# Twelve expert blocks moved into the attention stage, and the order of the loads fixed

## The chip, the cores and the metric

One core of one Trainium2 chip. The metric is the device time of the whole program in microseconds (us). A time quoted for a kernel is the median of its runs.

The engines are named as in the profile: PE is TensorE, PEld its weight loads, DVE is VectorE, ACT is ScalarE, POOL is GpSimd, SP is SyncE. The "granted clock" of a stretch is the share of TensorE's full clock that the profile records as let through: 1.00 is full, 0.50 is half. L144 is line 144 of that kernel's file, so the same operation has another line number in each kernel; go by the names of the tiles.

## The reference, cut to what matters

```python
# attention: batch 8, heads 8, sequence 576, head size 64
scores = scale * q @ k.T                      # per batch and head
scores = where(0 <= i - j < 128, scores + alibi_bias, -1e9)
x = (softmax(scores) @ v)  -> reshaped to (4608 tokens, 512)

# routing: 8 rounds that normalise rows and columns of P
P = exp(x @ w_gate - max)                     # (4608, 8)
for _ in range(8):
    P /= P.sum(1); P /= P.sum(0); P *= 4608 / 8

# every expert sees every token
for e in range(8):
    out += P[:, e:e+1] * (relu(x @ w1[e]) @ w2[e])   # 512 -> 1024 -> 512
```

Three properties carry the argument. An expert needs x, but not P, until its result is added up. P needs all tokens, because of the column sums. And the experts are by far the larger part: 8 experts x 4608 tokens.

## The kernel before

Loads. Each batch's q and k are cast to fp16 into a staging area in DRAM (three areas, used in turn), then read back transposed; v is cast straight into SBUF.

```python
def stage(b):
    sl = b % NST                                         # NST = 3
    nc.gpsimd.dma_start(out=q16[sl]..., in_=q[b]...)     # cast
    nc.gpsimd.dma_start(out=k16[sl]..., in_=k[b]...)     # cast
    vsb = asb.tile([P, NKB, H, Dh + 2], FP16, tag="vsb", bufs=3)
    for kb in range(NKB):
        nc.gpsimd.dma_start(out=vsb[0:nk, kb, :, 0:Dh], in_=v[b, ...])
    ...
    nc.sync.dma_start(out=QT, in_=q16[sl], transpose=True)
    nc.sync.dma_start(out=KT, in_=k16[sl], transpose=True)

stage(0); stage(1)
for b in range(B):
    if b + 2 < B: stage(b + 2)
    if b == B - 4: prefetch_weights(0)
    if b == B - 1: prefetch_weights(1)
    ...
```

The scheduler may reorder instructions within an engine's queue where data allow it, and it did so with these loads.

Attention, per batch and key block (five key blocks a batch; cut): 8 score matmuls of a 64-row array tile, exp on ScalarE, mask on VectorE, up to 16 value matmuls, division by the row sum, 4 transposes into `xT`; at the end of a batch the gate.

```python
for j in range(4):
    for hb in range(2):
        nc.tensor.matmul(out=ps[0:nk, hb, 0:nq], lhsT=KT[64*hb:64*hb+64, ...], rhs=QT[64*hb:64*hb+64, ...])   # psS
...
for i, (hh, lhsT, rhs) in enumerate(ops):
    nc.tensor.matmul(out=psN[0:nqb, hh, :], lhsT=lhsT, rhs=rhs, ...)
...
for dc in range(NDT):
    nc.tensor.matmul(out=psXT[:, dc, 0:nqb], lhsT=xsb[...], rhs=ident[...], is_transpose=True, ...)
```

Then the eight routing rounds (VectorE and GpSimd), then the experts: per expert nine blocks of 512 tokens, each 32 matmuls of the first layer (`psh`) and 32 of the second (`psy`), all 128x512, and the sum in `acc`:

```python
for e in range(E):
    for g in range(NG):
        ...                                    # psh -> relu on ACT -> hT; psy
        if e == 0: acc = psy * P_sb[:, blk, 0:1]          # VectorE
        else:      acc = psy * P_sb[:, blk, e:e+1] + acc  # VectorE
```

The softmax here doesn't subtract the row's maximum and nothing guards it: scores larger than these inputs give would overflow.

Of the kernel before, what the change touches and what calls it, by code (L numbers as in the profile page):

```python
# [9 lines left out]
FP16 = mybir.dt.float16  # L10
# [4 lines left out]
def kernel(  # L15
# [39 lines left out]
    NST = 3  # L55
    q16 = nc.dram_tensor("q16_i", [NST, S, HD], FP16, kind="Internal").ap()
    k16 = nc.dram_tensor("k16_i", [NST, S, HD], FP16, kind="Internal").ap()

    per = ctx.enter_context(tc.tile_pool(name="per", bufs=1))
    xT = per.tile([P, NDT, Ntok], FP16, name="xT")  # L60
    P_sb = per.tile([P, NBLK, E], FP32, name="P_sb")
# [14 lines left out]
    def prefetch_weights(e: int):  # L76
        w1t = per.tile([P, NDT, Fd], FP16, name=f"w1t_{e}", tag="w1t", bufs=2)
        w2t = per.tile([P, NFT, HD], FP16, name=f"w2t_{e}", tag="w2t", bufs=2)
        nc.gpsimd.dma_start(out=w1t, in_=moe_w1[e].rearrange("(dt p) f -> p dt f", p=P))  # L79
        nc.gpsimd.dma_start(out=w2t, in_=moe_w2[e].rearrange("(ft p) d -> p ft d", p=P))  # L80
        w1ts[e] = w1t
        w2ts[e] = w2t

    gate_done = 0

    with (
# [3 lines left out]
        staged: dict = {}  # L90

        def stage(b: int):
            sl = b % NST
            nc.gpsimd.dma_start(  # L94
                out=q16[sl].rearrange("s (h d) -> s h d", d=Dh),
# [3 lines left out]
                out=k16[sl].rearrange("s (h d) -> s h d", d=Dh),  # L99
                in_=k[b].rearrange("h s d -> s h d"),  # L100
            )
            vsb = asb.tile([P, NKB, H, Dh + 2], FP16, name=f"vsb_{b}", tag="vsb", bufs=3)
# [8 lines left out]
            QT = asb.tile([P, NDT, S], FP16, name=f"QT_{b}", tag="QT", bufs=3)  # L111
            KT = asb.tile([P, NDT, S], FP16, name=f"KT_{b}", tag="KT", bufs=3)
            nc.sync.dma_start(out=QT, in_=q16[sl], transpose=True)  # L113
            nc.sync.dma_start(out=KT, in_=k16[sl], transpose=True)
            staged[b] = (vsb, QT, KT)

        stage(0)
        stage(1)
        for b in range(B):
            if b + 2 < B:  # L120
                stage(b + 2)
            vsb, QT, KT = staged.pop(b)
            if b == B - 4:
                prefetch_weights(0)
            if b == B - 1:
                prefetch_weights(1)

            pt_prev = None
            for kb in range(NKB):
# [6 lines left out]
                for j in range(4):  # L136
# [12 lines left out]
                    psS.append(ps)  # L149

# [25 lines left out]

                xsb = asb.tile([P, H, Dh], FP16, name=f"xsb_{b}_{kb}", tag="xsb", bufs=2)
# [35 lines left out]
                psXT = aps.tile([P, NDT, P], FP16, name=f"psXT_{b}_{kb}", tag="psXT")  # L213
# [14 lines left out]
            for blk in range(gate_done, done):  # L228
                psG = aps.tile([P, E], FP32, name=f"psG_{blk}", tag="psG")
# [10 lines left out]

        for _ in range(8):
# [22 lines left out]
    with (  # L264
        tc.tile_pool(name="msb", bufs=1) as msb,
        tc.tile_pool(name="mps", bufs=1, space=bass.MemoryType.PSUM) as mps,
    ):
        acc = msb.tile([P, NBLK, HD], FP32, name="acc")
        for e in range(E):
            if 1 <= e and e + 1 < E:  # L270
                prefetch_weights(e + 1)
            w1t = w1ts[e]
# [3 lines left out]
            def emit_l1(g, e=e, w1t=w1t, hTs=hTs):  # L276
                hT = msb.tile([P, NFT, GT], FP16, name=f"hT_{e}_{g}", tag="hT", bufs=2)
                for ft in range(NFT):
                    psh = mps.tile([P, GT], FP32, name=f"psh_{e}_{g}_{ft}", tag="psh", bufs=2)
                    for dt in range(NDT):  # L280
                        nc.tensor.matmul(  # L281
                            out=psh,
                            lhsT=w1t[:, dt, P * ft : P * ft + P],
                            rhs=xT[:, dt, GT * g : GT * g + GT],
                            start=(dt == 0),
                            stop=(dt == NDT - 1),
                        )
                    nc.scalar.activation(out=hT[:, ft, :], in_=psh, func=AF.Relu)  # L288
                hTs[g] = hT

            def emit_l2(g, e=e, w2t=w2t, hTs=hTs):
                hT = hTs.pop(g)
                for ms in range(4):
                    blk = 4 * g + ms
                    psy = mps.tile([P, HD], FP32, name=f"psy_{e}_{blk}", tag="psy", bufs=3)
# [8 lines left out]
                    if e == 0:  # L304
                        nc.vector.tensor_scalar(  # L305
                            out=acc[:, blk, :],
                            in0=psy,
                            scalar1=P_sb[:, blk, 0:1],
                            scalar2=None,
                            op0=ALU.mult,  # L310
                        )
                    else:
                        nc.vector.scalar_tensor_tensor(  # L313
                            out=acc[:, blk, :],
                            in0=psy,
                            scalar=P_sb[:, blk, e : e + 1],
                            in1=acc[:, blk, :],
                            op0=ALU.mult,
                            op1=ALU.add,
                        )  # L320
# [6 lines left out]
            for g in range(NG):  # L327
                if g + 1 < NG:
                    emit_l1(g + 1)
                emit_l2(g)  # L330
# [30 lines left out]
```

## Time and profile before

| | |
|---|---|
| median of 4 runs | 1241.53 us (1238.02 to 1244.81) |
| profiled execution | span 1241.1 us |
| attention and loads | 0 to 229 us |
| routing rounds and the first expert blocks | 229 to 257 us |
| dense expert matmuls | to 1241 us, 216.2 ns each |

The prediction below shows the views that it rests on.

```profile
PE 1141.7 (92%) x5808; PEld 532.6 (43%) x5808; DVE 334.9 (27%) x704; ACT 427.4 (34%) x773; POOL 86.3 (7%) x85
...
L144 PE MATMUL psS<-QT,KT 64*128 64x256 f16 (+2 forms) x320 | 72.4, 349 | 41.9 <-DMA KT<-k_i 36.5
L195 PE MATMUL psN<-vsb,pt 128*128 128x65 f16 (+2 forms) x576 | 64.1, 246 | 46.3 <-DMA vsb<-in_v_dram 46.2
```

Keep two numbers in mind: PE is busy 1141.7 us with 5808 instructions, and a score matmul takes 349 ns on average.

### The profile page before, as it was taken

The page shows a single profiled execution, that of the slowest core. Times are in us where ns is not written, and L with a number is a line of the kernel's source. Part 1 is how long each engine was busy: PE and PEld are TensorE (multiplying, and loading weights), DVE is VectorE, ACT ScalarE, POOL GpSimd, SP SyncE. Part 2 cuts the span into 40 slices and gives each one's busy share as a digit, 9 for nine tenths or more (in the row PEclk, how much of TensorE's full clock was granted, in tenths as well). Part 3 has the DMA queues.
Part 4 walks back from the last instruction along what each step waited for, and adds up shares of the span by engine and source line. Part 5 has one row for each costly group of instructions (what it writes and reads, how often), then busy time and mean ns, then how long its engine had stood idle before and what let it go on. Part 6 is the DMA issues. An engine that isn't in the chain of part 4 may idle for free.

```text
span 1241.1 us, 13876 instructions
## 1 busy us (share of the span) xinstructions
PE 1141.7 (92%) x5808; PEld 532.6 (43%) x5808; DVE 334.9 (27%) x704; ACT 427.4 (34%) x773; POOL 86.3 (7%) x85
## 2 busy tenths in 40 slices
PE   0880589989999999999999999999999999999998
PEld 0450355434444444444444444444444444444443
DVE  0560366731221122112211221122111211121112
ACT  1440355423333333333233323332333233323331
POOL 6431330000000000000000000000000000000000
PEclk9999999989999999999999999999999999999999
DMA  9999995000040004000300030003100310001212
GB/s 146 153 154 139 157 146 25 2 1 1 1 67 2 1 1 62 8 1 1 58 11 1 1 55 14 1 1 49 20 1 1 47 23 1 1 1 60 77 68 102
DMA packets 167471, 51.27 MB, mean 41 GB/s; under 512 B 150384, under 2 KB 158576, under 8 KB 167408
## 3 DMA queue, kind: packets, MB, share of 16 engines
q0 software_dynamic: 124560, 30.95, 28.6%
q1 hardware_dynamic: 42848, 19.44, 9.2%
q8 instruction: 45, 0.74, 0.3%
q14 instruction: 18, 0.15, 0.0%
HBM read 62.44 MB, written 18.87 MB: 66 GB/s over the span
## 4 chain that ended last, share of the span: by engine, by line
PE 84%; DMA 9%; DVE 2%; issue 2%; ACT 1%; POOL 1%; SPq 0%; DVEq 0%; POOLq 0%; ACTq 0%
PE psy L297 40%; PE psh L281 39%; DMA vsb<-in_v_dram 7%; PE psS L144 2%; PE psN L195 2%; DMA q_i<-in_q_dram 2%; PE psXT L215 1%; DMA KT<-k_i 1%; ACT e L156 1%; SPq L113 0%; DVE cs_sb L250 0%; PE psG L231 0%; DVE P_sb L244 0%; DVE rs_sb L242 0%; POOL ca_sb L253 0%
## 5 line engine op out<-in xcount | busy, mean ns | idle before, releaser
L288 ACT ACTIVATE hT<-psh 128x512 f16<-128x512 f32 x576 | 343.8, 597 | 650.9 <-PE psh L281 635.4
L297 PE MATMUL psy<-w2t,hT 128*128 128x512 f16 x2304 | 510.4, 380 | 5.8 <-DVE acc L305 5.8
L281 PE MATMUL psh<-xT,w1t 128*128 128x512 f16 x2304 | 512.9, 380 | 0.4 <-ACT P_sb L238 0.3
L313 DVE SCALAR_TENSOR_TENSOR acc<-psy,P_sb,acc 128x512 f32<-128x512 f32 x252 | 189.2, 751 | 683.9 <-PE psy L297 683.9
L297 PEld LDWEIGHTS <-hT 128*128 128x128 f16 x2304 | 225.4, 98 | 279.7 <-issue 8.5
L281 PEld LDWEIGHTS <-w1t 128*128 128x128 f16 x2304 | 225.1, 98 | 277.7 <-issue 14.6
L156 ACT ACTIVATE e<-psS 128x512 f16<-128x512 f32 (+2 forms) x160 | 77.2, 510 | 106.6 <-PE psS L144 96.4
L144 PE MATMUL psS<-QT,KT 64*128 64x256 f16 (+2 forms) x320 | 72.4, 349 | 41.9 <-DMA KT<-k_i 36.5
L195 PE MATMUL psN<-vsb,pt 128*128 128x65 f16 (+2 forms) x576 | 64.1, 246 | 46.3 <-DMA vsb<-in_v_dram 46.2
L195 PEld LDWEIGHTS <-pt 128*128 128x128 f16 (+2 forms) x576 | 44.3, 132 | 69.8 <-issue 56.4
L169 DVE TENSOR_TENSOR pt<-e,maskT 128x512 f16<-128x512 f16 (+2 forms) x160 | 52.5, 355 | 28.4 <-ACT e L156 28.3
L79 POOL DMA_DIRECT2D w1t<-in_moe_w_dram x8 | 6.6, 826 | 648.4 <-PE psh L281 645.3
L305 DVE TENSOR_SCALAR acc<-psy,P_sb 128x512 f32<-128x512 f32 x36 | 26.8, 750 | 82.2 <-PE psy L297 81.8
L144 PEld LDWEIGHTS <-KT 64*128 64x128 f16 (+1 forms) x320 | 22.4, 106 | 56.9 <-DMA KT<-k_i 36.9
L106 POOL DMA_DIRECT2D vsb<-in_v_dram x40 | 35.7, 1053 | 49.2 <-DMA q_i<-in_q_dram 16.6
L224 DVE COPY xT<-psXT 128x512 f16<-128x512 f16 (+1 forms) x40 | 15.9, 398 | 73.6 <-PE psS L144 51.3
L206 DVE TENSOR_TENSOR xsb<-psN,rden 128x256 f16<-128x256 f32 (+1 forms) x80 | 31.3, 408 | 0.1
L215 PE MATMUL psXT<-ident,xsb 128*128 128x128 f16 (+1 forms) x160 | 30.2, 290 | 0.8 <-DVE xsb L206 0.8
L205 DVE RECIPROCAL rden<-psN 128x4 f32<-128x4 f32 (+1 forms) x80 | 14.1, 177 | 27.7 <-PE psN L195 27.5
L98 POOL DMA_DIRECT2D k_i<-in_k_dram x8 | 18.1, 2263 | 32.6 <-issue 17.6
L94 POOL DMA_DIRECT2D q_i<-in_q_dram x8 | 17.9, 2244 | 26.7 <-issue 18.7
L238 ACT ACTIVATE P_sb<-psG 128x8 f32<-128x8 f32 x36 | 6.4, 177 | 38.4 <-PE psG L231 37.6
(18 smaller groups left out, 64.0 us busy)
## 6 DMA issues: line engine op xcount, KB each, us to landing
out_dram<-acc SPq DMA_DIRECT2D x36, 256.0 KB, 2.0
w1t<-in_moe_w_dram POOLq DMA_DIRECT2D x8, 1024.0 KB, 8.2
w2t<-in_moe_w_dram POOLq DMA_DIRECT2D x8, 1024.0 KB, 9.2
q_i<-in_q_dram POOLq DMA_DIRECT2D x8, 576.0 KB, 20.6
k_i<-in_k_dram POOLq DMA_DIRECT2D x8, 576.0 KB, 19.3
vsb<-in_v_dram POOLq DMA_DIRECT2D x32, 128.0 KB, 18.6
maskT<-maskT_c SPq DMA_DIRECT2D x1, 512.0 KB, 3.3
vsb<-in_v_dram POOLq DMA_DIRECT2D x8, 64.0 KB, 17.8
```

What stands on the lines that cost most here:

```text
L106: nc.gpsimd.dma_start(out=vsb[0:nk, kb, :, 0:Dh], in_=v[b, :, k0 : k0 + nk, :].rearrange("h s d -> s h d"),)
L144: nc.tensor.matmul(out=ps[0:nk, hb, 0:nq], lhsT=KT[64 * hb : 64 * hb + 64, j, k0 : k0 + nk], rhs=QT[64 * hb : 64 * hb + 64, j, k0 : k0 + nq],)
L156: nc.scalar.activation(out=e4[0:nk, :, 0:nq], in_=psS[j][0:nk, :, 0:nq], func=AF.Exp, scale=scale,)
L169: nc.vector.tensor_tensor(out=ptj[0:nk, :, 0:nq], in0=e4s[j][0:nk, :, 0:nq], in1=maskT[0:nk, 2 * j : 2 * j + 2, 0:nq], op=ALU.mult,)
L195: nc.tensor.matmul(out=psN[0:nqb, hh, :], lhsT=lhsT, rhs=rhs, start=(i == 0), stop=(i == len(ops) - 1),)
L206: nc.vector.tensor_tensor(out=xsb[0:nqb, 4 * hg : 4 * hg + 4, :], in0=psN[0:nqb, :, 0:Dh], in1=rden[0:nqb, :].unsqueeze(2).to_broadcast([n ...
L215: nc.tensor.matmul(out=psXT[:, dc, 0:nqb], lhsT=xsb[0:nqb, 2 * dc : 2 * dc + 2, :], rhs=ident[0:nqb, 0:nqb], is_transpose=True, start=(dc ...
L281: nc.tensor.matmul(out=psh, lhsT=w1t[:, dt, P * ft : P * ft + P], rhs=xT[:, dt, GT * g : GT * g + GT], start=(dt == 0), stop=(dt == NDT - 1),)
L288: nc.scalar.activation(out=hT[:, ft, :], in_=psh, func=AF.Relu)
L297: nc.tensor.matmul(out=psy, lhsT=hT[:, ft, P * ms : P * ms + P], rhs=w2t[:, ft, :], start=(ft == 0), stop=(ft == NFT - 1),)
L305: nc.vector.tensor_scalar(out=acc[:, blk, :], in0=psy, scalar1=P_sb[:, blk, 0:1], scalar2=None, op0=ALU.mult,)
L313: nc.vector.scalar_tensor_tensor(out=acc[:, blk, :], in0=psy, scalar=P_sb[:, blk, e : e + 1], in1=acc[:, blk, :], op0=ALU.mult, op1=ALU.add,)
```

## The change

The intent: during attention the DMA engines are the bottleneck and PE waits; afterwards PE is the bottleneck. So expert work that needs no P yet is run inside the attention stage, and the loads are put in an order in which none is late. Its parts:

- The loads are split into `stage_cast`, `stage_xbar` (transposes) and `stage_v`; GpSimd's queue keeps program order; each batch has its own staging area; Q, K and V have two buffers instead of three; the weights of experts 0 and 1 are loaded early.
- All nine blocks of expert 0 and three of expert 1 are queued in pieces (8 pieces of 4 first-layer matmuls, 4 pieces of 8 second-layer matmuls a block) and issued by `fill()` at three places in each key block.
- Expert 0's results go into `acc` unscaled and are scaled later; the three early blocks of expert 1 go to DRAM in fp16 and come back at the end of expert 1.
- Transposes, gate and both expert layers share two PSUM buffers in this stage.

```diff
+        def fill():
+            n = -(-len(pending) // max(1, slots_left[0]))
+            slots_left[0] -= 1
+            for _ in range(n):
+                pending.pop(0)()
...
+        pool_order.enter_context(
+            tc.manual_schedule(engines={mybir.EngineType.Pool})
+        )
+        stage_cast(0)
+        stage_v(0)
+        stage_xbar(0)
+        stage_cast(1)
+        stage_xbar(1)
+        stage_v(1)
+        prefetch_weights(0)
         for b in range(B):
             if b + 2 < B:
-                stage(b + 2)
-            vsb, QT, KT = staged.pop(b)
-            if b == B - 4:
-                prefetch_weights(0)
-            if b == B - 1:
+                stage_cast(b + 2)
+            if 0 < b and b + 1 < B:
+                stage_xbar(b + 1)
+                stage_v(b + 1)
+            if b == 1:
                 prefetch_weights(1)
+            slots_left[0] = 3 * NKB
...
                     psS.append(ps)
+                fill()
...
                     pt_cur.append(ptj)
+                fill()
...
+                fill()
-                psXT = aps.tile([P, NDT, P], FP16, name=f"psXT_{b}_{kb}", tag="psXT")
+                psXT = aps.tile([P, NDT, P], FP16, name=f"psXT_{b}_{kb}", tag="pmm", bufs=2)
...
+            for g in range(ovl_done, ng_done):
+                queue_block(0, g)
+            if b - 2 in e1_early:
+                queue_block(1, b - 2)
+        slots_left[0] = 1
+        fill()
```

(The pieces themselves are the expert code shown above with `nc.vector.tensor_copy(out=acc[:, 4 * g + ms, :], in_=psy)` for expert 0.)

`fill()` rounds up, so 12 pieces in 15 places fill the first 12 and leave the last three, the last key block, empty.

## The prediction

> **What bounds the kernel now**
>
> I read the strip of forty slices first, then PE's (TensorE's) waits, then the busy time stage by stage, and last the order of PE's own stream inside the attention stage.
>
> The strip, of which these are the rows for PE, PoolE and the DMA engines (busy tenths, 31 us a slice):
>
> ```profile
> PE   0880589989999999999999999999999999999998
> POOL 6431330000000000000000000000000000000000
> DMA  9999995000040004000300030003100310001212
> ```
>
> The kernel has two halves. For 190 us the sixteen DMA engines are full and PE is not; from slice 8 on PE is full and the DMA engines are nearly empty. Each half leaves idle what the other half is short of. The second half is 1000 us long, so an overlap can win at most PE's gaps in the first.
>
> PE's waits in the first 260 us (engine, line, what it waited for, us in total, times, longest):
>
> ```profile
> PE psN L195 <- DMA vsb<-in_v_dram: 46.2, 3, 37.6
> PE psS L144 <- DMA KT<-k_i: 36.5, 4, 28.4
> PE psy L297 <- DVE acc L305: 5.8, 1, 5.8
> ```
>
> Three gaps: the first transposed K (28.4 us of the 36.5, before anything can start), V tiles that come late (one wait of 37.6 us in the middle of batch 4), and 5.8 us in which the first expert's results wait for the routing weights.
>
> The stages (window, its length, then busy us and instruction count of PE, weight load, VectorE, ScalarE, GpSimd, then granted clock, mean DMA engines' share, GB/s):
>
> ```profile
> 0.00:28.36 28.36, 0.00 (x1) 0.01 (x2) 0.31 (x3) 1.28 (x1) 18.40 (x19) 1.00 1.71 145
> 28.36:47.92 19.56, 13.54 (x114) 7.46 (x114) 9.48 (x32) 9.98 (x22) 8.60 (x7) 1.00 1.94 151
> 47.92:67.34 19.42, 17.49 (x148) 10.20 (x148) 12.16 (x46) 10.21 (x24) 6.58 (x3) 1.00 1.96 157
> 67.34:92.74 25.40, 22.95 (x191) 13.34 (x192) 15.24 (x60) 12.54 (x31) 11.74 (x9) 1.00 1.88 154
> 92.74:130.68 37.94, 0.31 (x4) 0.25 (x3) 0.41 (x2) 0.35 (x1) 5.87 (x4) 1.00 1.84 143
> 130.68:176.00 45.32, 35.35 (x302) 20.91 (x301) 24.31 (x92) 20.59 (x49) 17.21 (x17) 1.00 1.96 152
> 176.00:229.38 53.38, 50.06 (x445) 30.07 (x444) 35.97 (x136) 28.58 (x70) 4.89 (x6) 1.00 0.62 43
> 229.38:257.08 27.70, 21.95 (x96) 9.57 (x96) 21.75 (x50) 9.55 (x16) 3.18 (x8) 0.98 0.00 1
> 600.00:800.00 200.00, 200.00 (x925) 90.11 (x924) 44.30 (x59) 67.46 (x113) 3.27 (x4) 1.00 0.14 22
> 1200.00:1241.10 41.10, 37.25 (x173) 16.58 (x170) 10.51 (x14) 9.55 (x16) 0.00 (x0) 1.00 0.25 96
> ```
>
> Taking PE's busy time from each length, PE idles 28.4 + 6.0 + 1.9 + 2.5 + 37.6 + 10.0 + 3.3 = 89.7 us before the experts start, 5.8 us after, and 3.9 us at the end. The row for 600 to 800 us gives the rate of dense expert matmuls: 200 us / 925 = 216.2 ns. One expert block of 512 tokens has 64 of them: 13.84 us. All 72 blocks: 4608 x 216.2 ns = 996 us.
>
> One batch of attention, where nothing waits for a transfer, takes PE 18 us: two successive windows of 18 us, from 176 to 212 us, hold 40 score matmuls each, which is one batch, and PE is busy 17.3 and 17.5 us of them. A piece of that stream shows why (start, length, engine, line, operation, array tile, shape, count):
>
> ```profile
> 57.95 0.39 PE L144 MATMUL psS<-QT,KT 64*128 64x256 f16 x1
> 58.27 0.29 PE L195 MATMUL psN<-vsb,pt 128*128 128x65 f16 x2
> 58.50 0.39 PE L144 MATMUL psS<-QT,KT 64*128 64x256 f16 x1
> 58.82 0.40 PE L215 MATMUL psXT<-ident,xsb 128*128 128x128 f16 x2
> 59.01 0.43 PE L195 MATMUL psN<-vsb,pt 128*128 128x65 f16 x4
> ```
>
> A score matmul (64*128 array tile) sits between 128*128 ones, and the next instruction starts 0.32 us after it, although four times as many value matmuls pass in 0.36 us. So "busy" here is not throughput: the stream alternates between two array shapes about 40 times a batch.
>
> **What the Trainium skill says**
>
> "TensorEngine Tiling (Array Packing)", section Key Properties: changing the tiling mode drains the TensorE. The trace agrees, with the 0.32 us steps above. Expert matmuls are of the 128*128 kind, so they add switches only where they split a run of scores.
>
> "TensorE: Matmul & The Clock Gate", section "Wait — 56ns, not 53.3ns?": 215.7 ns start to start for 512 columns when warm. The trace has 216.2 ns, so the 996 us can't be compressed, only begun earlier.
>
> "DMA: Bandwidth & Descriptors", section "Issuing engines are not separate DMA queues": all queues share the same 16 engines. The trace agrees: the software queue and the transposes together keep them full at about 150 GB/s. Ordering therefore decides who waits; volume doesn't change.
>
> "ScalarE: Activation LUTs", section "Table sets: the hidden batching unit": relu is in every table set. The trace agrees: ScalarE's 773 instructions are 160 + 576 + 36 activations and a single table load of 1.28 us, so mixing exp and relu costs no reload.
>
> **The change, part by part**
>
> 1. Transfer order. GpSimd now issues in program order, weights of expert 0 after batch 1, of expert 1 after V of batch 2, each V just ahead of its batch, and each batch has its own staging tensor. Before, the weights and the casts of later batches were issued ahead of V of batch 4, which made the 37.6 us gap. The volume is the same, about 28.5 MB. Per batch it is five times 0.59 MB (two casts, V, two transposes), 2.95 MB at 157 GB/s: 18.8 us. A weight pair is 2.1 MB and runs at about 205 GB/s when alone: 10 us. So: batch 0 starts at 28.4 and batch 1 at 48 us as now; the weights of expert 0 take the place of batch 2's casts and land near 48 to 52; two pairs of casts (7.5 us each), the transposes and V make batch 2 ready near 75; weights 1 and batch 3 near 100.
>
> 2. Fill. Twelve blocks move into attention's slots: nine of expert 0, three of expert 1. Block 0 runs in batch 1, block 1 in batch 2, two blocks each in batches 3, 4, 5, one each in 6 and 7, two after the last batch. A batch then costs PE 18 + 13.84 = 31.8 us, or 45.7 with two blocks. Batch 1 would run from 48 to 80, batch 2 to 112: later than 75 and 100, when their successors are ready. From batch 1 on, PE no longer waits for data. This also hides the shrinking from three to two buffers of Q, K and V: the 19 us from the start of a transpose pair to its landing are shorter than a batch.
>
> 3. The routing iterations (229 to 256 us now) have 27.5 us of queued blocks plus two first-layer blocks and three results of expert 1 ahead of them, 46 us of PE work: the 5.8 us wait goes.
>
> 4. Added work. VectorE: 36 copies instead of 36 scalings (now 750 ns each), then 36 scalings and 12 more accumulations; about 48 x 0.75 = 36 us over a stage in which VectorE is some 22% busy. ScalarE and VectorE stay at 10 + 9.6 and 12 + 6 us of a 45 us batch. The 12 stores and 3 loads of partial results (1.6 MB each way) go over idle DMA engines. None of it is on PE's path.
>
> Sum for PE: 996.2 (experts) + 8 x 18.0 = 144 (attention) + 28.4 (first K) + 5.2 (K of batch 1; the gap of 5.2 us ahead of 47.92 stays) + 3 (an allowance, an estimate, for the first block waiting for its weights) + 3.9 (the end) = 1180.7. From the other side: 1241.1, less the removed idle time: of 89.7 us stay 28.4, 5.2 and 0.6 in each of eight batches, so 51 go, with 5.8 more: 1184. I take **1180 us**, 5% faster, as the fill should hide part of the 0.6 us gaps.
>
> **Rivals**
>
> A. Attention gets cheaper inside the mix. Summing steps within runs, I estimate 11 us of a batch's 18 as pure matmul issue, and the rest as switches and gaps. If the fill keeps score matmuls together, a batch could cost 14 to 15: 8 x 3.5 = 28 us less, 1152. Against it: scores are issued in pairs as their PSUM buffers (one of each kind) come free after an exp of 0.6 us, so pairs will still be split, now by expert matmuls. I lean to no change.
>
> B. Queues in order turn the fill into a new wait. PE can't pass a first-layer matmul whose weights have not landed, ScalarE can't pass a store that waits for a VectorE copy, and the transposes, the gate and both expert layers share two PSUM buffers, so a transpose can wait for a relu behind four exps. Say 0.5 us in each of 40 key blocks: +20 us, 1200. For it: single buffers for scores. Against: PE has twice the work to hide latencies, and the dense stage runs without loss on two buffers with the same 597 ns relu.
>
> C. DMA remains the bound. If casts, transposes and weights came no faster than 190 us for all, fills would be starved. Against it: PE's work in the mix (8 x 18 + 138 = 282 us of PE time before the last fill) is much longer than 190 us. It only matters for batches 1 to 3; worst case 20 us, 1200.
>
> D. The late weights or the partial results stall expert 1: its last 12 accumulations need up to 14 us of VectorE, against 13.8 us of first-layer work ahead on PE. Worth 0 to 3 us.
>
> **Range and chances**
>
> A pulls by up to 28 us down, B and C by 20 up each, and they are unlikely to come together: 1158 to 1204 for 8 in 10. Faster by 2% means under 1216.7, which needs 37 us of new waits: faster 0.95, same 0.04, slower 0.01.
>
> **What would show it**
>
> Right: in the strip, PE at 9 from slice 2 or 3 on; no PE wait for V over a few us; the wait of the first results for routing weights gone; DMA spread over more slices at a lower share; the first expert matmul near 50 us; routing iterations later than now, near 320 to 350 us; the dense stage unchanged at 216 ns. Wrong: PE waits for exps, for PSUM evacuation or for weights that add up to over 20 us between 50 and 330 us (B, C), or batches that take clearly less than 31.8 us with one block (A).

## The result, and the profile after

| | before | after |
|---|---|---|
| median | 1242.75 us (16 runs) | 1158.87 us (11 runs, 1155.98 to 1161.63) |
| ratio | 1 | 0.9325 [0.9306, 0.9344] |
| span of the profiled execution | 1241.1 us | 1160.2 us |

A ratio here and below is the mean time of one kernel's fast runs over that of the other's from the same rounds, so it is not quite the ratio of the medians quoted. The before of each ratio was run beside the kernel on the same chip.

The gain is 84 us, where 61 was predicted (1241.5 to 1180). The time lies inside the predicted range, at its lower edge: 0.9 us above 1158. The sum was 21 us too high, and the parts of it missed by more, in both directions.

The strip of the changed kernel (forty slices of 29 us; busy tenths):

```profile
PE   0599999999899999999999999999999999999998
...
DMA  9999996050140220004000400022001300001112
```

PE is at 9 from slice 2 on, where before it fell to 0 in slice 3 (counted from 0). PE's waits over the whole execution (what waits, what it waited for, us in total, times, longest):

```profile
PE psS L253 <- DMA KT<-k: 41.0, 2, 28.3
...
PE psy L155 <- DVE acc L163: 2.5, 2, 1.6
PE psh L107 <- DVE acc L163: 1.7, 1, 1.7
PE psS L253 <- ACT e L266: 1.6, 7, 0.5
```

The 46.2 us for V are gone, and so are the 5.8 us for the routing weights; the 41.0 us for K are the first load (28.3) and one more wait, 12.7 us, ahead of batch 1. So the waits did about what was expected of them. But now the page's groups, the same lines as those shown of before:

```profile
PE 1102.8 (95%) x5808; PEld 506.3 (44%) x5808; DVE 363.9 (31%) x752; ACT 421.6 (36%) x773; POOL 86.8 (7%) x85
...
L253 PE MATMUL psS<-QT,KT 64*128 64x256 f16 (+2 forms) x320 | 47.8, 276 | 43.5 <-DMA KT<-k 41.0
...
L306 PE MATMUL psN<-vsb,pt 128*128 128x65 f16 (+2 forms) x576 | 38.2, 203 | 0.2
```

PE is busy 39 us less with the same 5808 instructions. An overlap alone only moves work; it does not make it shorter. Score matmuls fell from 349 to 276 ns, value matmuls from 246 to 203 ns.

The stages (window, length, then busy us and count of PE, weight load, VectorE, ScalarE, GpSimd, granted clock, DMA share, GB/s). Each of the first eight windows is one batch, from its first score matmul; the ninth is the last fill with the routing rounds, the tenth the dense stage:

```profile
28.28:55.21 26.93, 13.23 (x107) 7.06 (x107) 9.48 (x32) 9.91 (x20) 7.50 (x4) 1.00 1.61 175
55.21:85.86 30.65, 30.13 (x226) 14.94 (x227) 17.50 (x57) 14.12 (x32) 12.44 (x10) 1.00 1.90 166
85.86:113.65 27.79, 27.44 (x217) 13.54 (x216) 16.44 (x52) 14.33 (x34) 8.61 (x7) 0.88 1.91 160
113.65:155.43 41.78, 41.60 (x286) 19.73 (x287) 19.90 (x61) 19.14 (x41) 10.17 (x9) 0.92 1.42 110
155.43:194.46 39.03, 37.69 (x283) 18.32 (x284) 19.39 (x54) 18.84 (x41) 8.66 (x8) 1.00 0.96 90
194.46:234.99 40.53, 39.00 (x280) 18.58 (x280) 19.38 (x54) 18.64 (x40) 4.22 (x6) 0.96 0.45 60
234.99:261.31 26.32, 25.48 (x209) 12.55 (x209) 15.92 (x45) 14.07 (x33) 2.70 (x4) 0.94 0.47 48
261.31:289.30 27.99, 26.44 (x245) 14.18 (x245) 17.95 (x57) 14.87 (x37) 0.00 (x0) 1.00 0.01 2
289.30:324.50 35.20, 30.17 (x132) 12.88 (x131) 30.30 (x69) 9.73 (x17) 5.16 (x10) 0.95 0.32 75
600.00:800.00 200.00, 199.84 (x925) 89.98 (x923) 43.30 (x58) 68.62 (x115) 3.27 (x4) 1.00 0.14 22
```

Take the 12.74 us wait off the first window, and 13.84 us for each expert block off the others (1, 1, 2, 2, 2, 1, 1 of them). What is left is attention's own share of each batch: 14.2, 16.8, 14.0, 14.1, 11.4, 12.9, 12.5, 14.2; together 109.9 us. Predicted: 8 x 18.0 = 144. (The single shares are rough: the scheduler moves work across these borders, and of a batch's 150 attention matmuls the first window holds 107 and the last about 180. The sum is not affected.) In the dense stage nothing changed: 200 us / 925 = 216.2 ns.

Why does an expert block make attention cheaper? PE's timeline inside batch 2 and at its end (start, length, engine, line, operation, array tile, shape, count):

```profile
86.25 0.28 PE L253 MATMUL psS<-QT,KT 64*128 64x256 f16 x1
86.46 0.31 PE L306 MATMUL psN<-vsb,pt 64*64 64x65 f16 x4
86.70 0.28 PE L253 MATMUL psS<-QT,KT 64*128 64x256 f16 x1
86.91 0.25 PE L306 MATMUL psN<-vsb,pt 64*64 64x65 f16 x2
...
89.01 0.39 PE L253 MATMUL psS<-QT,KT 64*128 64x256 f16 x1
89.33 0.27 PE L343 MATMUL psG<-wg_sb,xT 128*128 128x8 f16 x4
89.54 0.39 PE L253 MATMUL psS<-QT,KT 64*128 64x256 f16 x1
89.86 0.27 PE L343 MATMUL psG<-wg_sb,xT 128*128 128x8 f16 x4
```

The same instruction, a lone score matmul among others: at 86 us the next one starts 0.21 us after it, at 89 us 0.32 us after it, which is the step that the prediction read in the kernel before. The array switches shape in both places. What differs is how long ago PE did dense work. The kernel before has the decisive lines too, at the place where attention ends and the first expert matmuls begin (its PE weight loads, one for each matmul):

```profile
229.76 0.15 PEld L281 LDWEIGHTS <-w1t 128*128 128x128 f16 x1 [0.27 <-issue]
230.19 0.15 PEld L281 LDWEIGHTS <-w1t 128*128 128x128 f16 x1 [0.28 <-issue]
230.61 0.15 PEld L281 LDWEIGHTS <-w1t 128*128 128x128 f16 x1 [0.28 <-issue]
231.04 0.15 PEld L281 LDWEIGHTS <-w1t 128*128 128x128 f16 x1 [0.28 <-issue]
```

They are 0.43 us apart: twice the 0.216 us of the dense stage. At the end of attention PE ran at half clock, although it had been busy with no pause over half a microsecond, and although the granted clock of that window reads 1.00.

That 1.00 is a blank and not a measurement. The packed trace holds each change of the clock. In the kernel before, the first one is a rise to full clock at 232.0 us, 2.6 us after the first expert matmul, and the view counts the time ahead of the first change as full. All fourteen traces here begin with a rise; in the changed kernel it comes at 68.2 us. After it the record and the steps agree: in the changed kernel the step after a lone 64x256 score matmul has a median of 0.21 us at recorded full clock (28 of them) and 0.32 us at half clock or ahead of the first rise (14), and the median of the 70 in the kernel before is 0.32 us too.

Theory: in the kernel before, PE's clock is halved during attention, because its stream of small matmuls doesn't count as dense work; the filled-in expert matmuls keep it up. Main rival: the clock plays no part, and the fill saves switches, because score matmuls get grouped. The switches speak against it from the start, though not altogether. By the array tile that each record names, PE's stream changes shape 379 times before and 290 times after. (The expectations below count only changes between scores and other matmuls, 323 and 273; in the order of the traces these are 323 and 279.) At about 0.1 us each (worked out below), 89 changes fewer are an estimated 9 us of the 34: a part of the gain, but not most of it.

### The profile page after: what moved, and what is told of

Same layout as the page of the kernel before. It is cut to its first block, busy times and chain, and to the rows that moved or that the text cites.

```text
span 1160.2 us, 13915 instructions
## 1 busy us (share of the span) xinstructions
PE 1102.8 (95%) x5808; PEld 506.3 (44%) x5808; DVE 363.9 (31%) x752; ACT 421.6 (36%) x773; POOL 86.8 (7%) x85
## 4 chain that ended last, share of the span: by engine, by line
PE 90%; DMA 4%; DVE 3%; POOL 1%; ACT 1%; issue 1%; SPq 0%; ACTq 0%; DVEq 0%; POOLq 0%
PE psh L107 36%; PE psy L420 36%; PE psh L141 7%; PE psy L155 6%; PE psS L253 2%; PE psN L306 2%; DMA KT<-k 2%; DMA q<-in_q_dram 2%; PE psXT L327 1%; DMA ysp<-ysbuf 1%; SPq L198 0%; DVE acc L163 0%; PE psG L343 0%; DVE acc L411 0%; DVE cs_sb L372 0%
## 5 line engine op out<-in xcount | busy, mean ns | idle before, releaser
L107 PE MATMUL psh<-xT,w1t 128*128 128x512 f16 x1920 | 425.6, 379 | 1.8 <-DVE acc L163 1.7
L427 DVE SCALAR_TENSOR_TENSOR acc<-psy,P_sb,acc 128x512 f32<-128x512 f32 x240 | 180.2, 751 | 635.1 <-PE psy L420 635.1
L141 PE MATMUL psh<-xT,w1t 128*128 128x512 f16 x384 | 106.5, 417 | 1.3 <-DVE acc L163 0.9
L253 PE MATMUL psS<-QT,KT 64*128 64x256 f16 (+2 forms) x320 | 47.8, 276 | 43.5 <-DMA KT<-k 41.0
L279 DVE TENSOR_TENSOR pt<-e,maskT 128x512 f16<-128x512 f16 (+2 forms) x160 | 56.3, 366 | 46.5 <-ACT e L266 43.0
L253 PEld LDWEIGHTS <-KT 64*128 64x128 f16 (+1 forms) x320 | 16.7, 97 | 62.7 <-DMA KT<-k 41.2
L207 POOL DMA_DIRECT2D vsb<-in_v_dram x40 | 35.8, 1071 | 107.9 <-PE psN L306 96.7
L306 PE MATMUL psN<-vsb,pt 128*128 128x65 f16 (+2 forms) x576 | 38.2, 203 | 0.2
L306 PEld LDWEIGHTS <-pt 128*128 128x128 f16 (+2 forms) x576 | 29.1, 105 | 18.7 <-issue 7.2
L163 DVE COPY acc<-psy 128x512 f32<-128x512 f32 x36 | 24.8, 690 | 24.6 <-PE psy L155 24.6
L316 DVE RECIPROCAL rden<-psN 128x4 f32<-128x4 f32 (+1 forms) x80 | 12.9, 173 | 48.6 <-PE psN L306 48.3
## 6 DMA issues: line engine op xcount, KB each, us to landing
q<-in_q_dram POOLq DMA_DIRECT2D x8, 576.0 KB, 16.8
```

The lines of the kernel that those rows point to most:

```text
L107: nc.tensor.matmul(out=psh, lhsT=w1t[:, dt, P * ft : P * ft + P], rhs=xT[:, dt, GT * g : GT * g + GT], start=(dt == 0), stop=(dt == NDT - 1),)
L141: nc.tensor.matmul(out=psh, lhsT=w1t[:, dt, P * ft : P * ft + P], rhs=xT[:, dt, GT * g : GT * g + GT], start=(dt == 0), stop=(dt == NDT - 1),)
L207: nc.gpsimd.dma_start(out=vsb[0:nk, kb, :, 0:Dh], in_=v[b, :, k0 : k0 + nk, :].rearrange("h s d -> s h d"),)
L253: nc.tensor.matmul(out=ps[0:nk, hb, 0:nq], lhsT=KT[64 * hb : 64 * hb + 64, j, k0 : k0 + nk], rhs=QT[64 * hb : 64 * hb + 64, j, k0 : k0 + nq],)
L279: nc.vector.tensor_tensor(out=ptj[0:nk, :, 0:nq], in0=e4s[j][0:nk, :, 0:nq], in1=maskT[0:nk, 2 * j : 2 * j + 2, 0:nq], op=ALU.mult,)
L427: nc.vector.scalar_tensor_tensor(out=acc[:, blk, :], in0=psy, scalar=P_sb[:, blk, e : e + 1], in1=acc[:, blk, :], op0=ALU.mult, op1=ALU.add,)
```

## The experiments

All twelve gave correct results. They start from the changed kernel, except e9_before_heat, which starts from the kernel before.

### 1. The order of the loads without the fill

```diff
         def fill():
-            n = -(-len(pending) // max(1, slots_left[0]))
-            ...
+            return
+        def flush():
+            while pending: pending.pop(0)()
...
         # after the last batch
-        fill()
+        flush()
```
(Here and in experiments 2 and 3, each block's `hT` tile is now allocated with its first piece.)

> The changed kernel with its transfer order, but all twelve expert blocks run after the last batch instead of inside attention. It shows what the transfer order is worth alone. From the prediction's own numbers: the transfers need about 190 us, the last batch about 18 us more, then 72 blocks of 13.84 us (996 us) and an end of 4 us: 1208 us, and 1205 to 1225 as two buffers of Q and K couple the transposes to the batches. If the order were all that mattered it would stay near the 1159 us of the changed kernel. Attention steps should look as in the kernel before: 0.32 us from a lone score matmul to the next instruction.

Measured: 1220.70 us, ratio 0.9831 [0.9804, 0.9858]. The order, with all else but the fill, is worth 20 us, the fill the other 62. The page's score matmuls and PE's waits:

```profile
L260 PE MATMUL psS<-QT,KT 64*128 64x256 f16 (+2 forms) x320 | 68.0, 349 | 66.5 <-DMA KT<-k 61.6
```

```profile
PE psS L260 <- DMA KT<-k: 61.6, 8, 28.5
...
PE psN L313 <- DMA vsb<-in_v_dram: 2.8, 1, 2.8
```

The wait for V falls from 46.2 to 2.8 us, but the wait for K grows from 36.5 to 61.6: without expert work PE is ahead of the transfers at every batch. And the score matmuls are back at 349 ns, to the nanosecond the mean of the kernel before, although by array tile this run has 333 changes of shape, 46 fewer. So the faster attention comes with the fill, not with the order, the single PSUM tag or the buffers. The fill does two things: of the 59 us between the two spans (1219.5 and 1160.2), 23 are waits for K and V that it covers (61.6 + 2.8 - 41.0), and most of the rest is the shorter attention.

### 2. The fill in one lump at the end of each batch

```diff
             if b - 2 in e1_early:
                 queue_block(1, b - 2)
+            flush()
```
(with `fill()` empty as above)

> The same blocks at the same places between batches, but each as one lump after a batch, not spread through the next one. PE has the same work, the transfers the same order. Clock theory (PE runs the attention at half clock when nothing dense is near, and the spread fill keeps it at full clock): a batch costs 18 us again plus 1.7 us for a lump that starts at half clock, against 13.7 us in the changed kernel: 7 x 6 = 42 us more, about 1201 us, with 0.32 us steps. Grouping theory (the fill saves changes of the array shape): PE's order here has 293 changes between score and other matmuls, the changed kernel 273, the kernel before 323; 20 of 50 of the 34 us gained: about 1172 us.

Measured: 1191.33 us, ratio 0.9595 [0.9566, 0.9624]: between the two theories, nearer to the clock's 1201 than to 1172. The timeline shows why it is between. A lump ends at 110.94 us, attention follows:

```profile
111.27 0.28 PE L260 MATMUL psS<-QT,KT 64*128 64x256 f16 x1
111.49 0.43 PE L313 MATMUL psN<-vsb,pt 128*128 128x65 f16 x8
...
118.84 0.39 PE L260 MATMUL psS<-QT,KT 64*128 64x256 f16 x1
119.16 0.29 PE L313 MATMUL psN<-vsb,pt 128*128 128x65 f16 x2
```

The step is 0.22 us right after the lump and 0.32 us eight us later, in one batch and with no fill anywhere near. Here the records show it as well. Windows of the lump's end, the attention of the next batch, and the first part of the next lump (the granted clock is the number after GpSimd's):

```profile
99.72:110.94 11.22, 11.22 (x53) 5.06 (x52) 2.08 (x3) 3.58 (x6) 4.38 (x2) 1.00 2.07 156
110.94:126.29 15.35, 14.73 (x149) 8.86 (x148) 11.58 (x44) 9.49 (x24) 3.06 (x4) 0.68 1.63 157
126.29:135.04 8.75, 8.75 (x34) 3.60 (x34) 1.18 (x4) 4.63 (x8) 5.61 (x4) 0.79 1.95 125
```

0.68 in attention, though PE is busy 14.73 of 15.35 us: the clock falls while PE works. It comes up again in the lump, whose first 32 matmuls take 8.91 us instead of 7.07 in the warm run of the next experiment. The attention of this batch costs 15.35 + 1.8 us, between the 18 of before and the 11.4 of the best batch after. I had expected the clock to fall at once. By the trace's record it fell here at 116.4 us, and over the seven lumps 5.1 to 8.3 us after a lump's end; that is a reason why the lump came out 10 us under the clock theory's 1201.

### 3. The lump, with dummy matmuls in the places of the fill

```diff
         def fill():
-            return
+            ph = aps.tile([P, GT], FP32, name=f"heat_{next(heat_no)}", tag="pmm", bufs=2)
+            for _ in range(2):
+                nc.tensor.matmul(out=ph, lhsT=maskT[:, 0, 0:P], rhs=maskT[:, 0:2, :], start=True, stop=True)
```

> The lump kernel with two dummy matmuls of 128x512 at each of the 15 places of a batch where the changed kernel has its fill; their results go nowhere. They are 240 x 216 ns = 52 us of extra PE work. Clock theory: they keep the clock up, a batch's own matmuls take 12 to 13 us instead of 18, and the lumps start warm: within 10 us of the lump kernel despite the extra work, with steps of 0.21 us after a lone score matmul. Any theory without the clock: the lump kernel's time plus about 50 us.

Measured: 1208.52 us, ratio 0.9735 [0.9703, 0.9767]: 17 us over the lump. The 240 dummies are 52 us of work at 0.216 us each. So two thirds of the added work came back. (About 6 of these 35 us are dummies that ran while PE waited for transfers: it waited 41.4 us for K in the lump, here 31.1 us for K and 4.1 us for the dummies' own operand.) The clock theory allowed up to 10 us more, the rival asked for 50. The timeline and the window of the same batch as above:

```profile
110.83 0.28 PE L267 MATMUL psS<-QT,KT 64*128 64x256 f16 x1
111.04 0.39 PE L188 MATMUL heat<-maskT 128*128 128x512 f16 x1
```

```profile
108.26:126.43 18.17, 17.82 (x179) 9.07 (x179) 14.06 (x46) 9.28 (x24) 4.51 (x4) 1.00 1.48 118
```

The granted clock is 1.00 for the whole batch, and 18.17 us less 30 dummies x 0.216 = 11.7 us for attention. Dense work in the stream, of no use to anything, makes the attention beside it a third shorter than the 18 us of before. It also answers the grouping rival: by array tile there are 355 changes of shape in the lump and 322 with the dummies, and 33 changes at 0.1 us are 3 us in the whole kernel, where this one batch became 3.7 us shorter (15.35 to 11.7).

### 4. The scheduler's own order on GpSimd

```diff
-        pool_order.enter_context(
-            tc.manual_schedule(engines={mybir.EngineType.Pool})
-        )
```

> The changed kernel without the fixed order of transfers on GpSimd; the compiler then puts the casts of batches 4 to 7 ahead of V of batch 3 and the weights of expert 1 ahead of V of batch 2. PE's order is the same, instruction by instruction. If PE's work sets the time once the fill is there, a late V costs little: eight casts of 3.8 us are 30 us, of which about 15 us are slack, so 1160 to 1180 us with one wait for V of up to 20 us. If the order was the main gain, the 37.6 us wait comes back: 1195 us or more.

Measured: 1182.96 us, ratio 0.9532 [0.9504, 0.956], 24 us more than with the fixed order. PE's instructions stand in the same order in both. The scheduler puts the casts of batches 4 to 7 ahead of V of batch 3, and the one wait that comes of it carries the whole difference:

```profile
PE psN L303 <- DMA vsb<-in_v_dram: 24.0, 2, 23.3
```

So the fill doesn't make the order unimportant: while PE waits for V in program order, the expert pieces behind it wait too.

### 5. The weights of expert 0 one batch later

```diff
-        prefetch_weights(0)
         for b in range(B):
             if b + 2 < B:
                 stage_cast(b + 2)
+            if b == 0:
+                prefetch_weights(0)
```

> The changed kernel with the weights of expert 0 issued after the casts of batch 2 instead of before them. In the changed kernel PE waits 12.7 us for K of batch 1, whose transpose took 20.6 us to land beside those weights; in the kernel before it was 5.2 us and about 13 us. If the weights are what slows that transpose: 7 us less, 1152 us, and the wait back at about 5 us. If any traffic does: no change within 2 us, wait still 12 us.

Measured: 1155.80 us, ratio 0.9294 [0.9269, 0.9318], against 0.9325 for the changed kernel. The intervals overlap, so the gain of about 4 us is likely and not certain. The waits moved as meant: for K 32.6 instead of 41.0 us, with 3.3 us of waiting for the weights in exchange. So 8.4 of the 12.7 us ahead of batch 1 come from the weights of expert 0, issued beside K's transpose: it took 20.6 us to land in the changed kernel and 12.1 us here.

### 6. The pieces spread over all fifteen places

```diff
-            n = -(-len(pending) // max(1, slots_left[0]))
-            slots_left[0] -= 1
+            total, used = batch_total[0], batch_total[1]
+            batch_total[1] += 1
+            n = (used + 1) * total // slots_left[0] - used * total // slots_left[0]
```

> The changed kernel with each batch's expert pieces spread evenly over its 15 places; there the first 12 places have one piece each and the last three none. Clock theory: the stretch around each batch's end without dense matmuls (about 4 us, after which the clock drops and the next 3.4 us of expert matmuls run at half speed, 1.7 us lost) goes: about 7 x 1.5 us less, 1149 us, and the mean of a first-layer matmul falls from 417 to about 390 ns. Grouping theory: 279 changes of array shape against 273, so no gain, 1159 to 1162 us.

Measured: 1153.00 us, ratio 0.9269 [0.9243, 0.9294], some 7 us better than the changed kernel. It leaves no long stretch without dense work at a batch's end. The first-layer matmuls of the fill, the ones that start a batch's fill after that stretch, go from a mean of 417 to 402 ns; dense, they take 379. I had expected 1149 and 390: some cold starts remain. By the trace's record, the time at half clock between the first rise and the end of the last fill goes from 23.8 to 13.6 us. I had also counted seven batches with empty places, and there are four.

### 7. The last copies on ScalarE

```diff
-                if e == 0:
+                if e == 0 and g >= 7:
+                    nc.scalar.activation(out=acc[:, 4 * g + ms, :], in_=psy, func=AF.Copy)
+                elif e == 0:
                     nc.vector.tensor_copy(out=acc[:, 4 * g + ms, :], in_=psy)
```

> The changed kernel with the results of the last two blocks of expert 0 copied by ScalarE, idle there, instead of VectorE, which works on the routing iterations. PE waited about 5 us for those copies (waits on acc between 301 and 325 us). If that wait ends last: 4 to 5 us less, 1154 us. If the routing iterations end last in any case: no change.

Measured: 1154.66 us, ratio 0.9288 [0.9263, 0.9312], about 4.6 us better, as expected; the intervals overlap slightly. PE's waits for VectorE's copies into `acc` (2.5 + 1.7 + 0.9 us in the changed kernel) are gone, but for one of 0.7 us for ScalarE's. In VectorE's timeline of the changed kernel those copies stand among routing rounds and scalings.

### 8. Nine blocks instead of twelve

```diff
-    e1_early = (0, 1, 2)
+    e1_early = ()
```

> The changed kernel without the early blocks of expert 1 and their trip through memory: nine blocks of fill, not twelve. The prediction's sum has PE's work fixed, so it says no change (1159 us, or 2 us less for the gate's waits on the stored results). Clock theory: batches with two blocks ran their own work in about 12.8 us, those with one in about 14 us, so about 1.3 us more in each of three batches: 1161 to 1164 us. A theory in which the fill hides transfer waits would give far more, as three batches are 13.8 us shorter: up to 20 us.

Measured: 1161.09 us, ratio 0.9338 [0.9312, 0.9364]. The difference from the changed kernel, 1 to 2 us, is inside the intervals. The three blocks of expert 1, with their way through DRAM, are worth next to nothing here; this run doesn't tell the first two theories apart, and speaks against the third, which had up to 20 us less. What it does show: the gain does not need twelve blocks. One block in every batch's stream is nearly enough.

### 9. The kernel before, with dummy matmuls

```diff
+        def heat():
+            ph = aps.tile([P, 512], FP32, name=f"heat_{next(heat_no)}", tag="psG")
+            nc.tensor.matmul(out=ph, lhsT=maskT[:, 0, 0:P], rhs=maskT[:, 0:2, :], start=True, stop=True)
...
+                for _ in range(2): heat()      # at three places in each key block
```

> The kernel before with two dummy matmuls of 128x512 at three places of each key block, 240 in all, 52 us of PE work at full clock. Only the last three batches (176 to 229 us) are not held up by transfers, so only there can they cost time. If the attention of the kernel before runs at half clock although its profile shows a granted clock of 1.00: the dummies lift the clock, a lone score matmul's step falls from 0.32 to 0.21 us, a dense batch takes 12 + 6.5 + 0.8 us (more changes of array shape) = 19 us against 18, and the total rises by 3 to 5 us at most, 1241 to 1247 us. If the clock was full and the 0.32 us were the drain alone: 3 x 7.3 = 22 us more, about 1263 us, and steps stay at 0.32 us.

Measured: 1263.22 us, ratio 1.0174 [1.0148, 1.02]. The time is that of the theory without a clock, 1263, and by the time alone my theory would have fallen. The trace, of the slowest of the four runs (1268.99 us), says otherwise. Two batches, whole, and a score matmul in the first of them:

```profile
187.04:212.14 25.10, 24.79 (x188) 11.91 (x187) 14.49 (x47) 10.82 (x27) 0.00 (x0) 0.77 0.55 54
212.14:233.63 21.49, 21.23 (x176) 10.37 (x175) 13.92 (x44) 9.49 (x24) 0.00 (x0) 0.90 0.01 2
```

```profile
195.47 0.28 PE L154 MATMUL psS<-QT,KT 64*128 64x256 f16 x1
195.68 0.39 PE L96 MATMUL heat<-maskT 128*128 128x512 f16 x1
```

Where the clock is up, the step is the warm 0.21 us here too. What I had wrong is the cost of the dummies. I took 30 x 0.216 = 6.5 us a batch; but the scheduler spread them, so that 215 of 240 stand alone, and one between scores takes a change of shape as well: 0.32 us where the clock is up, 0.54 where it isn't. In the second batch the steps of its thirty dummies add up to 9.0 us, and 12.5 us are left for attention, near the 11.7 of experiment 3. In the first the granted clock is 0.77 and the batch takes 25.1 us. So the dummies do raise the clock, not reliably, and at more cost than they bring. The expert matmuls of the change have to be run anyway.

### 10 to 12. A version that beats both

Experiment 10 puts the edits of 5, 6 and 7 together.

> Late weights of expert 0, evenly spread fill and ScalarE copies together, on the changed kernel. If their gains (by ratio 0.3, 0.6 and 0.4 per cent) are of different causes, they add: about 15 us less than the changed kernel, ratio to the kernel before near 0.920, 1143 us. If two of them share a wait: 1148 us or more.

Measured: 1160.99 us, ratio 0.9328 [0.9294, 0.9362], runs from 1153.93 to 1166.73: no better than the changed kernel, against an expected 1143. The gains didn't add up, because PE got ahead of the transfers again (timeline; in brackets the wait ahead of the instruction):

```profile
115.30 0.61 PE L261 MATMUL psS<-QT,KT 64*128 64x256 f16 x4 [7.45 <-DMA KT<-k]
...
122.06 0.27 PE L314 MATMUL psN<-vsb,pt 128*128 128x65 f16 x2 [4.78 <-DMA vsb<-in_v_dram]
```

Both waits are for batch 3. Its V stands behind two weight pairs, as in the changed kernel, but PE is ready for the batch at 107.9 us (115.30 - 7.45) and not at 113.7. This is the prediction's rival C. The trace is of one of the slowest runs (1166.62); its two waits are together 12.2 us, about the distance to the fastest run, which has no trace. Experiment 11 adds ten dummy matmuls at the start of batch 1, where they fall into the wait for the weights:

```diff
+            if b == 1:
+                pw = aps.tile([P, GT], FP32, name="warm", tag="pmm", bufs=2)
+                for _ in range(10):
+                    nc.tensor.matmul(out=pw, lhsT=xT[:, 0, 384:512], rhs=xT[:, 0, 0:512], start=True, stop=True)
```

> The same with ten dummy matmuls on PE just after the first score matmul of batch 1, on tokens of batch 0, so that batch 1 might begin at full clock: 10 x 427 ns cold = 4.3 us at most of added work. Clock theory: batch 1 runs its own work 2 to 4 us faster and its first expert matmuls lose 1.7 us less, so it comes out even or up to 2 us faster. Without the clock: 2 to 4 us slower.

Measured: 1154.95 us (1154.50 to 1155.22), ratio 0.9292 [0.9273, 0.9311]. The ten took 3.77 us, where ten warm ones take 2.16; the four first-layer matmuls after them took 1.03 us instead of 1.89. A cold start can thus be spent in a wait. Of the two waits for batch 3 one of 2.4 us for V is left in its trace; why the longer one went isn't shown. Experiment 12 mends the order of the loads itself, without the dummies: the weights of expert 1 are issued one batch later.

```diff
-            if b == 1:
+            if b == 2:
                 prefetch_weights(1)
```

> The combination of late weights of expert 0, evenly spread fill and ScalarE copies, which came out at 1154 or at 1160 to 1167 us because PE now reaches batch 3 before its K and V have landed (waits of 7.5 and 4.8 us), with one more move: the weights of expert 1, needed only in the second half of batch 3, are issued after V of batch 3 instead of before the casts of batch 4. They are 2.1 MB, about 10 us of transfers, so batch 3's data come about 10 us earlier. If the transfers ahead of batch 3 were what took the gains back: those waits go, the runs stop scattering, and the three gains add to 1141 to 1147 us. If something else did: 1153 us or more.

PE's longest waits in this version:

```profile
PE psS L261 <- DMA KT<-k: 32.6, 2, 28.4
PE psh L141 <- DMA w1t<-in_moe_w_dram: 3.2, 1, 3.2
```

Measured: 1148.15 us (1144.30 to 1150.91), ratio 0.9235 [0.9209, 0.9262]. The waits ahead of batch 3 are gone: of K only the first load and 4.2 us are left. It is the fastest version, 1.0% under the changed kernel (0.9235 / 0.9325 = 0.990), and just above the 1141 to 1147 that I expected. Its six runs still scatter over 6.6 us, and the scatter goes with the granted clock that was recorded for each: 0.993 or 0.994 in the three of 1149.70 us and more, 0.996 to 0.999 in the three of 1146.60 us and less. Why the clock was lower in some runs stays open.

## Why the prediction was right or wrong

The sum of the prediction against the profiled execution, which has a span of 1160.2 us:

| term | predicted | measured | difference |
|---|---|---|---|
| first K | 28.4 | 28.3 | -0.1 |
| K of batch 1 | 5.2 | 12.7 | +7.5 |
| first block waits for its weights | 3 | 0 | -3.0 |
| attention in eight batches | 144 | 109.9 | -34.1 |
| ten blocks inside the batches | 138.4 | 138.4 | 0 |
| two blocks after the last batch | 27.7 | 35.2 | +7.5 |
| sixty dense blocks | 830.4 | 830.4 | 0 |
| end | 3.9 | 5.3 | +1.4 |

(The three rows of blocks are the prediction's 996.2 us, split at 13.84 us a block. In the measured column the blocks are put at 13.84 us each, so attention's row holds whatever else the mix cost or saved; the last row is 1160.2 - 324.5 - 830.4.)

**The total: near, and partly by luck.** With attention at its measured size and nothing else changed, the sum would have been 1180.7 - 34.1 = 1146.6 us, below the range; the two terms that were 7.5 us too small brought the measured time back to its edge.

**The order of the loads: right.** The waits for V and the wait for the routing weights went, as said, and experiments 1 and 4 give the order a worth of 20 us without the fill and 24 us with it.

**The experts: right.** 216.2 ns in the dense stage, unchanged, and no block got cheaper than its matmuls.

**Attention: wrong, and this is the step that failed: "8 x 18.0 = 144 (attention)".** It measured 109.9 us. The prediction did look at the right lines: it read the 0.32 us step of a score matmul and asked why "busy" is not throughput. It answered that the array drains between two shapes, and cited a page that says so. The runs show that two thirds of that step is the matmul itself, at half clock: 256 columns are 0.107 us at the dense rate of 0.216 us for 512, twice that at half clock, and 0.32 - 0.213 and 0.21 - 0.107 both leave about 0.10 us for the switch. The switch is real, and its cost didn't change; the 0.107 us went. That it is the clock is shown four times over: by the steps sorted by the recorded clock, by the 0.43 us steps of the first expert matmuls in the kernel before, by the step that goes from 0.22 to 0.32 us within one batch of experiment 2 with a granted clock of 0.68, and by the dummies of experiment 3, which change little but how much dense work there is. Taken over all 1200 attention matmuls (from one start to the next, waits cut off at 0.6 us), the mean step is 124 ns before; after, it is 120 ns at half clock or ahead of the first rise (223 of them) and 69 ns at full clock. The 89 fewer changes of shape are the smaller part, an estimated 9 of the 34 us.

**Rival A: right in size and direction, wrong in its main cause.** It had "14 to 15" for a batch and 1152 for the time. I leaned away from it because I tied it to the grouping of scores, and found good reasons against grouping, which turned out to be the smaller part. Its 11 us of plain issue are near the 11.4 us of the best batch after, but by chance: they were summed from steps at half clock, and the 11.4 us contain the switches.

**K of batch 1: mis-sized by 7.5 us.** "The gap of 5.2 us ahead of 47.92 stays" left out that the weights of expert 0 are now issued ahead of where K's transpose ends. Experiment 5 moved them and got 8.4 us of that wait back. For the same reason the weights were early and their own allowance of 3 us wasn't used.

**The last fill: mis-sized by 7.5 us.** I had counted its matmuls only. It also has a cold start and waits on VectorE. The timeline of the changed kernel:

```profile
302.41 3.61 PE L155 MATMUL psy<-w2t,hT 128*128 128x512 f16 x16 [0.90 <-DVE acc L163]
306.19 1.02 PE L141 MATMUL psh<-xT,w1t 128*128 128x512 f16 x4 [0.17 <-DVE acc L163]
...
319.15 3.67 PE L155 MATMUL psy<-w2t,hT 128*128 128x512 f16 x16 [1.59 <-DVE acc L163]
```

The prediction said of the copies that "None of it is on PE's path"; these waits, with one of 0.68 and one of 1.68 us, are 5.0 us of exactly that, and experiment 7 took about as much away. The cold start is the rest, an estimate of 1.8 us from the lumps of experiments 2 and 3 (8.91 - 7.07).

**Rivals B and C.** B didn't happen: waits for exps and for shared PSUM buffers are a few us. C shows in the changed kernel only as the longer wait for K of batch 1, and in experiment 10 at batch 3 too.

Of the marks that the prediction set: PE at 9 from slice 2, no wait for V, no wait for routing weights, DMA over more slices and the dense stage unchanged all came; the first expert matmul at 62.7 us instead of near 50 and the routing rounds at 290 to 317 instead of 320 to 350 us are the K wait and the shorter attention; "batches that take clearly less than 31.8 us with one block (A)" is what the page shows from batch 2 on (27.8, 26.3, 28.0).

Why attention's share differs from batch to batch (11.4 to 16.8 us) can be read from the recorded clock. The batch from 155 us on has no half clock and 11.4 us. The next two have 3.4 us of it each and 12.9 and 12.5 us; those from 86 and 114 us have 6.8 us and 14.0 and 14.1; the one from 55 us has 13 us, until the first rise, and 16.8. That is roughly 11.4 us and half the time at half clock. The first batch ran ahead of the first rise: 14.2 us for 107 of its 150 matmuls. The last has no half clock, and 14.2 us for about 180.

What isn't settled: at what mix of small and dense work the clock falls.

## What to carry to other kernels

A PE row at 90% or more doesn't say that PE is at full speed: compare the step of the same matmul in two places, and look at the first dense matmuls after a stretch of small ones, before calling a cost a property of the shapes. Dense work that must be done anyway is worth more inside a stage of small matmuls than behind it, because it shortens its neighbours; dummy work cost more than it brought here (17 us in experiment 3, 21 us in experiment 9). A granted clock of 1.00 ahead of the first recorded change says nothing. And once PE has become faster, check the order of the loads again, for the bound goes back to them.

## What the Trainium skill lacked or had wrong

- "TensorE: Matmul & The Clock Gate", section "What's actually happening", has the clock fall after an idle window of about 3.4 us and rise after a busy one, and the advice at the page's end is to avoid idle gaps. Here it was half while PE was busy 17.3 to 17.5 us of each 18 with no pause over half a microsecond: the small matmuls (64x256, 128x65, transposes) did not bring it up. Two later sections come nearer: in the one on psum-queue depth-cycling short pauses make the clock swing, and by Part 4 PE transposes don't count as busy in the same way. That score and value matmuls without long pauses are not enough stands in none. The two speeds themselves are as the page has them: 0.43 and 0.216 us for 512 columns.
- The same page gives no time for how long the clock holds when dense work turns into small work. In experiment 2 it held for 5.1 to 8.3 us after a lump's end, by the recorded changes.
- The same page, section "Seeing it yourself", warns that the clock's recorded events can be unreliable. Here they fit the steps (0.21 and 0.32 us), but no page says that the time ahead of the first event is blank and can read as full clock: in the kernel before it read 1.00 until 232.0 us, at steps of 0.32 and 0.43 us.
- "TensorEngine Tiling (Array Packing)", section Key Properties, says that a change of mode drains the array, without a figure. Here a lone matmul between two shapes took about 0.10 us beyond its columns, at either clock.
